# Attention and two mixers on one core: pairs 2 and 3 of q and k load into the buffers of pairs 0 and 1

## The chip, the core and the metric

The kernel runs on one core of one Trainium2 chip. The metric is device time in microseconds (us) of one launch, from setup to the last output byte. Before the change it is 679.75 us, the median of three runs (679.57 to 682.46). TensorE is called PE, VectorE DVE, ScalarE ACT, GpSimd POOL and SyncE SP, as in the profile.

## The reference

Three stages follow one another on an input of 4 batches, 8 heads, 576 positions and a head width of 64.

```python
# 1 attention: softmax over a sequence pooled by 4, plus softmax in a band
out_up    = np.repeat(sm_attn(q_d, k_d, v_d), 4, axis=2)    # q_d, k_d, v_d: means of 4 positions
out_local = np.matmul(softmax(where(abs(i - j) < 4, scale * q @ k.T, -1e9)), v)
x = out_up + out_local                                      # 4 x 576 x 512 when heads are joined
# 2 mixer: over positions, then over channels
u = x + (relu(x^T @ w_tok1) @ w_tok2)^T
x = u + relu(u @ w_ch1) @ w_ch2                             # 512 -> 1536 -> 512
# 3 mixer: a rotation by theta = x @ w_theta
y = w_tok_r @ (x * cos(theta)) + w_tok_i @ (x * sin(theta))
u = x + y;  result = u + relu(u @ w_ch)
```

## The kernel before

Two heads of one batch are a *pair*; pair n is batch n // 4 and heads 2(n % 4) and the next, so there are 16 pairs. Two pairs of a batch are a *quad* (eight of them). In tile names `qk_b_p` is the q and k of pair 4b + p.

For each pair the kernel loads q and k transposed (`load_pair`, L375, 582 KB, four buffers), pools them by 4 on DVE (`pool_pair`, L421 and L422), computes the band's scores on PE (`pair_local`: warm-up matmuls L315, mask L530, scores L533), takes the maximum and subtracts on DVE (L545, L546), exponentiates on ACT (L553), transposes on PE (L558), and multiplies with v (L568) and divides (L577 to L582). For each quad it pools v on POOL (`pool_values`, L396 loads it, L398 to L404 pool), computes pooled attention (`quad_front`: scores `sd` L434 and L443, maximum `mxd` L452 and L460, exponential `pd` L468 and L473, transposes `pdt` L477 and L482, product `od` L493 to L500, division L504 to L507), and writes the small result `ods` to DRAM and reads it back repeated (`od` L510, `ot` L511, then `xu` L516 and L519). L595 adds `xu` to the band's result `x`. The token mixer (`token_mix`, L598) follows for each quad. Weights arrive as 64-bit words, `raw`, and are cut into two 32-bit floats by ACT, DVE and POOL (`converted`, L187 to L223).

The attention and the token mixer take about the first 180 us; the channel mixer and the last stage fill the rest.

The order of the work is written out by hand. Each of the functions above is a generator that yields after a step; `ORDER` (L33) names one step after another, `P3` for the load of pair 3, `K3` for its pooling, `L3` for its band, `V1` and `F1` for quad 1, and so on, and each engine takes its instructions in that order. So SP also issues DMAs in that order, and a DMA that must wait for its buffer, or for one of eight completion semaphores that the loads take in turn, holds back every DMA behind it. The last stage, from L1136 on, is not in the table: there a scheduler sets the order, from its own estimate of when things are ready.

The four q-and-k buffers are taken in the order of the calls: pair 0, 1, 4 and 2 take one each, and pair 3, the fifth load, waits until pair 0 has been read by DVE and PE.

Of the kernel before, what the change touches and what calls it, by code (L numbers as in the profile page):

```python
# [12 lines left out]
F32 = mybir.dt.float32  # L13
# [17 lines left out]
FIRST = 1  # L31
ROWS = ((8, 9), (0, 2), (4, 6), (2, 3))
ORDER = """  # L33
G3 P0 G2 I*2 P1 G3 P4 G3 V0 P2 G3 K0 G3 G2 I G2 I L0*2 P3 K1 F0 W1 L0 F0 L1 L0 G3 F0 V0 L1*2 V0 L2 W0 G1 G0 G6 V1 G2
K2 V0 G2 F0 L1 F0 L2 K3 K4 L0 F0 L0 L2 L1 G2 F1 L2 L1 L0 F0 F1 G1*2 F1 V1 F0 P5 F0 W3 L0 F1 G5 G0 L1 G0 F1 K5 G6 F2 L1
G0 P6 W2 G5 G6 L3 V1 F2 V1 L3 G6 F2 F1 L3 G1 G4 F1 L2 P7 L5 L2 L5 F1 G1 L3 A0 V2 X0 A1 T0 L3 G1 L5 G0 L3 T0 G0 L2 G2
F1 G4 F2 G5 T0 K6 T0 V2 X2 L2 G6 W5 F2 K7 V2 L4*2 E0.0*2 T0 L4 V3 V2 A2 L3 E0.1 L5 G4 L4 W4 L5 G6 L5 G4 L3 X2 F3 G5 P8
P9 A3 G4 F2 G5 E0.1 T1 G4 G5 T0 F2 V3 L4 F3 F2 T0 L4 V3 X2 F3 L6 V3 L6 X7 T0 P11 L6 X2 X0 F3 K8 U0.0 L6 T0 X2 X0 U0.0
F3 L4 U0.0 V4 K9 F2 F3 X0 L6 L4 L6 T1 F4 U0.1 X0 F3 T1 L5 U0.1 X0 T1 U0.1 F4 X7 X4 V4 F3 T1 X7 F4 W6 L5 X7 E1.1 F4
E1.0 E1.1 L8 V4 L8 X7 E1.0 X1 A4 F4 T1 P10 A5 T1 X2 T2 L8 T1 U1.0*2 T2 T1 U1.0 X1 F3 L7 X7 L7 T2 X1 T2 X4 X5 K10 X1 L8  # L40
L6 U1.1*2 L7 T2 E2.0 U1.1 W7 X4 L7 V4 X1 L7 F4 W9 L7 L6 X4 E2.1 E2.0 C0 E2.1 T2 X1 L8 K11 X5 L7 T2 X5 L8 W8 L9*2 L7 X5
P13 T2 P12 L9 L10 C0 A6 F5 X4 C0 U2.0 L10 U2.0 X5 U2.0 C0 X3 F5 X6 F4 F5 C0 A7 F4 L10 T3 X4 F5 L9 V5 T3 H0.1 L8 U2.1
F5 T2 H0.1 H0.0 K12 T3 L9 U2.1 X5 C0 L9 U2.1 K13 F4 X6*2 L10 T3 X3 W13 H0.0 X6 H0.2 F6 E3.0*2 V5 P14 T3 F6 V5 H0.2 F6
C0 V6 V5 L8 X3 E3.1 L9 H0.3 F5 E3.1 X3 W10 L9 F6 X3 F5 L10 V6 A9 T3 F5 T3 V6 U3.0 L10 K14 T3 V6 U3.0 X6 U3.0 T3 H0.3
# [70 lines left out]
def kernel(  # L115
# [172 lines left out]
    sb1 = actx.enter_context(tc.tile_pool(name="a1", bufs=1))  # L288
    sb2 = actx.enter_context(tc.tile_pool(name="a2", bufs=2))
# [3 lines left out]
    def wide(name):  # L293
        return big.tile([128, 2, 512], F32, tag="big", name=name)
# [25 lines left out]
    def step(name, gen):  # L320
        gens[name] = gen
# [52 lines left out]

    def load_pair(n):  # L375
        b, p4 = divmod(n, 4)
        qk = sb2.tile([128, 2, S + 6], F32, tag="qk", name=f"qk_{b}_{p4}", bufs=4)
        sp.dma_start(qk, qkT[b, p4])
        loaded[n] = qk
        yield  # L380
# [141 lines left out]
    def pair_local(n):  # L522
# [426 lines left out]
    def lazily(f):  # L949
        yield from f()  # L950
# [190 lines left out]
    sb1 = ctx.enter_context(tc.tile_pool(name="c1p", reuse_waits="tile", bufs=1))  # L1141
    sb2 = ctx.enter_context(tc.tile_pool(name="c2p", reuse_waits="tile", bufs=2))
# [93 lines left out]
    T0, T1 = slice(0, HALF), slice(HALF, S)  # L1236
# [221 lines left out]
```

## Time and profile before

| What | Value |
|---|---|
| Runs | 679.75 us median of 3 (679.57, 679.75, 682.46) |
| Profiled execution | 679.18 us, span 677.4 us, mean granted PE clock 0.992 |
| PE busy | 655.6 us, 97% of the span |
| DVE busy | 519.8 us, 77% |
| ACT busy | 321.1 us, 47% |
| POOL busy | 100.1 us, 15% |
| DMA | 109.93 MB, mean 162 GB/s |
| First 101 us | PE busy 84.02, DVE busy 85.18, DMA engines 81% busy |

The profile is that of one execution. Start times are microseconds from the start of the span. A timeline row gives the start, the duration, the engine, the line, the operation and its tiles; in brackets stands the idle time before it and what ended that. "SPq" rows are the issue of a DMA, not its transfer: when a load landed is seen where an engine waited for it. PE's clock is given as a share of 2.4 GHz, so 0.50 is the lower of its two levels, 1.2 GHz. The page's shares are means over the whole span, and the change lies in the first 50 us, where no engine is busy all the time.

### The profile page before, as it was taken

The page shows a single profiled execution, that of the slowest core. Times are in us where ns is not written, and L with a number is a line of the kernel's source. Part 1 is how long each engine was busy: PE and PEld are TensorE (multiplying, and loading weights), DVE is VectorE, ACT ScalarE, POOL GpSimd, SP SyncE. Part 2 cuts the span into 40 slices and gives each one's busy share as a digit, 9 for nine tenths or more (in the row PEclk, how much of TensorE's full clock was granted, in tenths as well). Part 3 has the DMA queues.
Part 4 walks back from the last instruction along what each step waited for, and adds up shares of the span by engine and source line. Part 5 has one row for each costly group of instructions (what it writes and reads, how often), then busy time and mean ns, then how long its engine had stood idle before and what let it go on. Part 6 is the DMA issues. An engine that isn't in the chain of part 4 may idle for free.

```text
span 677.4 us, 17394 instructions
## 1 busy us (share of the span) xinstructions
PE 655.6 (97%) x7320; PEld 625.6 (92%) x7320; DVE 519.8 (77%) x952; ACT 321.1 (47%) x632; POOL 100.1 (15%) x92
## 2 busy tenths in 40 slices
PE   7779889999999999999999999999999999999997
PEld 4658879989999999999999999999999998998997
DVE  5989988697542888998987867677898748847837
ACT  3566758355342564535434523154647227427311
POOL 3224222415000423300101200012000000000000
PEclk8889999999999999999999999999999999999999
DMA  8797877757343685527263762699510330140202
GB/s 294 235 300 236 269 248 250 254 184 233 105 147 126 221 294 187 202 65 214 57 195 128 206 142 85 236 323 277 141 63 0 106 121 1 62 142 1 71 1 70
DMA packets 93021, 109.93 MB, mean 162 GB/s; under 512 B 46880, under 2 KB 69536, under 8 KB 92944
## 3 DMA queue, kind: packets, MB, share of 16 engines
q1 hardware_dynamic: 92080, 106.08, 49.4%
q0 software_dynamic: 864, 2.75, 1.1%
q8 instruction: 57, 0.93, 0.6%
q14 instruction: 20, 0.16, 0.1%
HBM read 79.13 MB, written 29.69 MB: 161 GB/s over the span
## 4 chain that ended last, share of the span: by engine, by line
PE 84%; DMA 5%; DVE 5%; SPq 2%; ACT 2%; issue 1%; DVEq 0%; ACTq 0%
PE y L157 6%; PE y L158 6%; PE y L159 6%; PE c L158 4%; PE c L157 4%; PE c L159 4%; PE c L699 4%; PE c L702 4%; PE c L700 4%; PE c_p L902 3%; PE c_p L905 3%; PE c_p L903 3%; PE th L158 2%; PE th L159 2%; PE th L157 2%; DMA qk<-qkT 2%
## 5 line engine op out<-in xcount | busy, mean ns | idle before, releaser
L158 PE MATMUL y<-wrl,zh 128*128 128x288 f32 x256 | 74.9, 296 | 0.0
L157 PE MATMUL y<-wrh,zh 128*128 128x288 f32 x256 | 74.8, 296 | 0.0
L159 PE MATMUL y<-wrh,zl 128*128 128x288 f32 x256 | 71.9, 295 | 0.0
L219 POOL TENSOR_TENSOR ww<-ww,raw 128x512 int32<-128x512 int32 (+2 forms) x30 | 41.0, 1373 | 160.1 <-DMA raw<-w_ch 52.9
L157 PEld LDWEIGHTS y<-wrh,zh 128*128 128x128 f32 x256 | 48.0, 188 | 0.0
L158 PEld LDWEIGHTS y<-wrl,zh 128*128 128x128 f32 x256 | 48.0, 188 | 0.0
L159 PEld LDWEIGHTS y<-wrh,zl 128*128 128x128 f32 x256 | 46.9, 188 | 0.0
L219 POOL TENSOR_TENSOR raw<-raw 128x512 int32<-128x512 int32 (+2 forms) x16 | 20.4, 1275 | 133.5 <-DVE raw L215 57.6
L1231 DVE TENSOR_TENSOR cx<-y,cx 128x288 f32<-128x288 f32 x32 | 14.6, 456 | 32.3 <-PE y L159 31.8
L151 ACT CAST cuh<-cx 128x288 fp32r<-128x288 f32 (+1 forms) x16 | 8.8, 553 | 59.6 <-DVE cx L1231 59.6
L199 ACT ACTIVATE ww<-raw 128x512 f32<-128x512 f32 (+2 forms) x30 | 19.5, 649 | 27.4 <-DVE c1l L223 9.5
L157 PE MATMUL th<-thh,cxh 128*128 128x512 f32 (+1 forms) x92 | 31.6, 343 | 0.0
L158 PE MATMUL th<-thl,cxh 128*128 128x512 f32 (+1 forms) x92 | 31.6, 343 | 0.0
L159 PE MATMUL th<-thh,cxl 128*128 128x512 f32 (+1 forms) x92 | 31.1, 343 | 0.0
L921 DVE SCALAR_TENSOR_TENSOR g<-c,g 128x384 fp32r<-128x384 f32 x40 | 21.1, 549 | 12.8 <-ACT g L918 12.8
L918 ACT ACTIVATE g<-c 128x384 fp32r<-128x384 f32 x40 | 19.2, 490 | 24.4 <-PE c L159 24.4
L201 ACT ACTIVATE raw<-raw 128x512 int32<-128x512 uint32 (+3 forms) x46 | 29.5, 641 | 0.0
L929 DVE TENSOR_TENSOR ut<-c,ut 128x384 f32<-128x384 f32 x32 | 17.1, 550 | 9.9 <-PE c L702 9.9
L568 PE MATMUL o<-vw,plt 38*32 38x65 f32 x1280 | 18.0, 231 | 3.8 <-issue 3.1
L157 PE MATMUL t<-w2h,h 128*128 128x256 f32 (+1 forms) x64 | 21.5, 337 | 0.0
L157 PE MATMUL c<-uh,c1h 128*128 128x384 f32 x64 | 21.4, 334 | 0.0
L159 PE MATMUL c<-uh,c1l 128*128 128x384 f32 x64 | 21.4, 334 | 0.0
(390 smaller groups left out, 2256.7 us busy)
## 6 DMA issues: line engine op xcount, KB each, us to landing
raw<-w_ch SPq DMA_DIRECT2D x27, 512.0 KB
qk<-qkT SPq DMA_DIRECT2D x16, 582.0 KB
xT<-ut SPq DMA_DIRECT2D x12, 768.0 KB
vd<-vtok SPq DMA_DIRECT2D x8, 650.0 KB
vw<-vloc SPq DMA_DIRECT2D x32, 146.2 KB
uT<-us SPq DMA_DIRECT2D x16, 288.0 KB
ut<-uT SPq DMA_DIRECT2D x6, 768.0 KB
ut<-xT SPq DMA_DIRECT2D x6, 768.0 KB
```

The costliest lines, as they stand in the source:

```text
L157: pe.matmul(out, lh, rh, start=start, stop=False, skip_group_check=again)
L158: pe.matmul(out, lh, rl, start=False, stop=False, skip_group_check=again)
L159: pe.matmul(out, ll, rh, start=False, stop=stop, skip_group_check=again)
L201: act.activation(f, words[:, :, 0], AF.Copy, scale=2.0**-29)
L219: pool.tensor_tensor(out=w.bitcast(I32), in0=w.bitcast(I32), in1=f, op=ALU.add)
L699: pe.matmul(ps[:, 0:MIX], h[:, cb % 2, d], h1, start=cb == cbs[0], stop=False)
L700: pe.matmul(ps[:, 0:MIX], l[:, cb % 2, d], h1, start=False, stop=False)
L702: pe.matmul(ps[:, 0:MIX], weight[cb // 2][2][:, cb % 2, d], h2, start=False, stop=cb == cbs[-1])
L902: pe.matmul(ps[:, 0:MIX], h[:, cb % 2, d], h1, start=cb == cbs[0], stop=False)
L903: pe.matmul(ps[:, 0:MIX], l[:, cb % 2, d], h1, start=False, stop=False)
L905: pe.matmul(ps[:, 0:MIX], weight[cb // 2][2][:, cb % 2, d], h2, start=False, stop=cb == cbs[-1])
L921: dve.scalar_tensor_tensor(out=h2, in0=ps, scalar=0.0, in1=h1.bitcast(F32), op0=ALU.max, op1=ALU.subtract)
```

## The change

The q-and-k buffers become four tiles of their own, and a table says which pair uses which. Pairs 2 and 3 now use the buffers of pairs 0 and 1; pairs 4 and 5 use the other two, which nothing used before them. The table of steps is changed with it, in its first lines only.

```diff
-G3 P0 G2 I*2 P1 G3 P4 G3 V0 P2 G3 K0 G3 G2 I G2 I L0*2 P3 K1 F0 W1 L0 F0 ...
+G3 P0 G2 I*2 P1 G3*2 V0 G3 K0 G3 G2 I G2 I L0*2 P2 W0 G1 K1 F0 L0 F0 L1 L0 G3 F0 V0 L1 P3 G0 W1 ...
...
+QK = (0, 1, 0, 1, 2, 3, 0, 1, 3, 2, 3, 0, 2, 1, 3, 0)
...
-        qk = sb2.tile([128, 2, S + 6], F32, tag="qk", name=f"qk_{b}_{p4}", bufs=4)
+        qk = sb1.tile([128, 2, S + 6], F32, tag=f"qk{QK[n]}", name=f"qk_{b}_{p4}")
```

Line numbers of the kernel after are one higher from L92 on. The first place is SP's start, before: `qk_0_1` is pair 1, `qk_1_0` pair 4, `vd` the v of a quad, `vw` the v of a pair's band, `raw` a weight.

```order
L378 DMA qk_0_1_148<-qkT 128x1164
L378 DMA qk_1_0_152<-qkT 128x1164
L396 DMA vd_0_0_157<-vtok 128x1300
L378 DMA qk_0_2_159<-qkT 128x1164
L378 DMA qk_0_3_240<-qkT 128x1164
L387 DMA vw_0_1_266<-vloc 32x1170 x2
L387 DMA vw_0_1_266<-vloc 6x1170 x2
L387 DMA vw_0_0_364<-vloc 32x1170 x2
L387 DMA vw_0_0_364<-vloc 6x1170 x2
L187 DMA raw_2_369<-w_tok1 128x2x256
L187 DMA raw_3_371<-w_tok1 128x2x256
```

And the same stretch of SP after:

```order
L379 DMA qk_0_1_148<-qkT 128x1164
L397 DMA vd_0_0_155<-vtok 128x1300
L379 DMA qk_0_2_236<-qkT 128x1164
L388 DMA vw_0_0_238<-vloc 32x1170 x2
L388 DMA vw_0_0_238<-vloc 6x1170 x2
L188 DMA raw_2_243<-w_tok1 128x2x256
L379 DMA qk_0_3_342<-qkT 128x1164
L188 DMA raw_3_344<-w_tok1 128x2x256
L388 DMA vw_0_1_346<-vloc 32x1170 x2
L388 DMA vw_0_1_346<-vloc 6x1170 x2
```

Pair 4 is gone from behind pair 1. Pair 2 now waits for the readers of pair 0, and pair 3 for those of pair 1, with `raw_3` and `vw_0_1` behind it.

The second place is SP at the first pooled result, `od` and `ot` out and `xu` back in, before:

```order
L396 DMA vd_0_1_375<-vtok 128x1300
L510 DMA od_0_0_57<-ods_0_0_567 4x32x256
L511 DMA ot_0_0_65<-ods_0_0_567 4x32x64
L378 DMA qk_1_1_589<-qkT 128x1164
L516 DMA xu_0_0_591<-od_0_0_57 128x1x1024
L519 DMA xu_0_0_591<-ot_0_0_65 64x1x256 x2
L387 DMA vw_0_3_595<-vloc 32x1170 x2
```

And after:

```order
L511 DMA od_0_0_57<-ods_0_0_557 4x32x256
L512 DMA ot_0_0_65<-ods_0_0_557 4x32x64
L397 DMA vd_0_1_578<-vtok 128x1300
L517 DMA xu_0_0_580<-od_0_0_57 128x1x1024
L520 DMA xu_0_0_580<-ot_0_0_65 64x1x256 x2
L379 DMA qk_1_0_585<-qkT 128x1164
L379 DMA qk_1_1_587<-qkT 128x1164
L188 DMA raw_4_589<-w_tok2 128x288
L388 DMA vw_0_3_591<-vloc 32x1170 x2
```

Pairs 4 and 5 and `raw_4` are now issued behind `xu`, and `xu` waits for `od` to reach DRAM. At the second pooled result the same is done to pair 7 (`qk_1_3`), the v of quad 2 and a weight, all now behind `xu_0_1`.

The third place is DVE behind the band result of pair 1 (`x_0_0`), before; `qa` and `qkd` are the two adds of a pooling.

```order
L421 TENSOR_TENSOR qa_1_1_670<-qk_1_1_589 128x576
L422 TENSOR_TENSOR qkd_1_0_446<-qa_1_1_670 128x288
L577 TENSOR_SCALAR rl_0_1_697<-o_0_1_623 128x10
L578 RECIPROCAL rl_0_1_697<-rl_0_1_697 128x10
L582 TENSOR_TENSOR x_0_0_603<-o_0_1_623,rl_0_1_697 128x2x5x64
L203 TENSOR_SCALAR ww_4_673<-ww_4_673 128x288
L206 TENSOR_SCALAR ww_4_673<-ww_4_673 128x288
L215 SCALAR_TENSOR_TENSOR ww_4_673<-raw_4_373,ww_4_673 128x288
L452 TENSOR_REDUCE mxd_1_0_732<-sd_1_0_676 128x4
L460 TENSOR_REDUCE mxd_1_0_732<-sd_1_0_676 64x1 x2
L545 TENSOR_REDUCE mx_0_3_816<-s_0_3_715 128x10
```

And after:

```order
L583 TENSOR_TENSOR x_0_0_599<-o_0_1_619,rl_0_1_669 128x2x5x64
L422 TENSOR_TENSOR qa_1_0_674<-qk_1_0_585 128x576
L423 TENSOR_TENSOR qkd_1_0_673<-qa_1_0_674 128x288
L422 TENSOR_TENSOR qa_1_1_677<-qk_1_1_587 128x576
L423 TENSOR_TENSOR qkd_1_0_673<-qa_1_1_677 128x288
L204 TENSOR_SCALAR ww_4_666<-ww_4_666 128x288
L207 TENSOR_SCALAR ww_4_666<-ww_4_666 128x288
L216 SCALAR_TENSOR_TENSOR ww_4_666<-raw_4_589,ww_4_666 128x288
L546 TENSOR_REDUCE mx_0_3_783<-s_0_3_694 128x10
```

Both poolings of quad 2 stand together behind `x_0_0`; pair 4's stood between those of pair 3 and `mx_0_2`. The maximum of quad 2 (`mxd_1_0`) moves behind the low half of `x_0_0` (L606, `xl_0_0`), its scores on PE behind the transposes of pair 3, and its exponential on ACT behind `raw_6`.

## Rows read from the trace of the kernel before

**Rows 1.** Windows: busy time and count by engine, PE clock, DMA share, GB/s

```profile
0.00:101.00 101.00, 84.02 (x2451) 67.62 (x2452) 85.18 (x164) 60.41 (x142) 32.95 (x35) 0.95 0.81 263
101.00:677.40 576.40, 571.56 (x4870) 557.98 (x4870) 434.65 (x789) 260.74 (x490) 67.13 (x57) 1.00 0.46 145
```

**Rows 2.** Timeline of DVE, 4 to 11 us: start, duration, work, idle before

```profile
5.63 1.19 DVE L421 TENSOR_TENSOR qa<-qk 128x576 f32<-128x576 f32 x1 [0.37 <-DMA qk<-qkT]
...
7.88 0.43 DVE L215 SCALAR_TENSOR_TENSOR raw<-raw 128x256 uint32<-128x256 uint32 x1
...
9.54 0.76 DVE L421 TENSOR_TENSOR qa<-qk 128x576 f32<-128x576 f32 x1 [1.24 <-DMA qk<-qkT]
```

**Rows 3.** Timeline of SP, 0 to 46 us: issues of DMAs

```profile
1.20 0.42 SPq L378 DMA_DIRECT2D qk<-qkT  x1
...
3.53 0.91 SPq L378 DMA_DIRECT2D qk<-qkT  x2
...
23.12 0.62 SPq L510 DMA_DIRECT2D od<-ods  x1
...
29.59 2.79 SPq L387 DMA_DIRECT2D vw<-vloc  x4
...
32.42 0.35 SPq L187 DMA_DIRECT2D raw<-w_tok  x1
...
38.06 0.58 SPq L510 DMA_DIRECT2D od<-ods  x1
...
44.22 1.20 SPq L519 DMA_DIRECT2D xu<-ot  x2
```

**Rows 4.** Timeline of PE, 11 to 18 us

```profile
11.99 2.89 PE L315 MATMUL s<-zero 128*128 128x320 bf16 x12
...
15.82 1.80 PE L315 MATMUL s<-zero 128*128 128x320 bf16 x12
```

**Rows 5.** Windows, columns as in group 1

```profile
12.00:14.00 2.00, 2.00 (x10) 1.18 (x9) 1.86 (x4) 1.02 (x4) 1.34 (x1) 0.50 1.02 368
```

**Rows 6.** Timeline of DVE, 18 to 23 us

```profile
18.25 0.76 DVE L421 TENSOR_TENSOR qa<-qk 128x576 f32<-128x576 f32 x1
...
20.71 0.55 DVE L545 TENSOR_REDUCE mx<-s 128x10 f32<-128x380 f32 x1
```

**Rows 7.** Timeline of DVE, 29 to 51 us

```profile
29.51 0.75 DVE L421 TENSOR_TENSOR qa<-qk 128x576 f32<-128x576 f32 x1
30.30 1.44 DVE L422 TENSOR_TENSOR qkd<-qa 128x288 f32<-128x288 f32 x1
...
32.84 0.38 DVE L203 TENSOR_SCALAR ww<-ww 128x288 f32<-128x288 f32 x1
...
33.98 0.75 DVE L452 TENSOR_REDUCE mxd<-sd 128x4 f32<-128x576 f32 x1
...
35.83 0.56 DVE L545 TENSOR_REDUCE mx<-s 128x10 f32<-128x380 f32 x1 [0.57 <-PE s L533]
...
40.17 0.69 DVE L223 TENSOR_TENSOR w1l<-raw,w1h 128x512 fp32r<-128x512 f32 x1 [0.67 <-ACT w1h L221]
...
45.00 0.75 DVE L421 TENSOR_TENSOR qa<-qk 128x576 f32<-128x576 f32 x1
45.79 1.63 DVE L422 TENSOR_TENSOR qkd<-qa 128x288 f32<-128x288 f32 x1
...
48.52 0.83 DVE L421 TENSOR_TENSOR qa<-qk 128x576 f32<-128x576 f32 x1
...
50.32 0.42 DVE L643 SCALAR_TENSOR_TENSOR h<-t,h 128x256 fp32r<-128x256 f32 x1 [0.48 <-ACT h L640]
```

**Rows 8.** Timeline of POOL, 45 to 47 us

```profile
45.77 1.34 POOL L398 TENSOR_TENSOR vd<-vd 128x650 f32<-128x650 f32 x1 [9.52 <-DMA vd<-vtok]
```

**Rows 9.** Timeline of ACT, 30 to 36 us

```profile
35.09 0.48 ACT L199 ACTIVATE ww<-raw 128x288 f32<-128x288 f32 x1 [4.25 <-DMA raw<-w_tok]
```

**Rows 10.** Chain that ended last, a load of one pair later on

```profile
127.51 7.42 DMA qk<-qkT
```

More of the change, by code (lines that the diff above doesn't have):

```diff
@@ L33 @@
 ORDER = """
[L34 to L41, printed above, removed]
+G3 P0 G2 I*2 P1 G3*2 V0 G3 K0 G3 G2 I G2 I L0*2 P2 W0 G1 K1 F0 L0 F0 L1 L0 G3 F0 V0 L1 P3 G0 W1 L1 V0 L2 G2 K2 V0 G2
+F0 L1 F0 L2 K3 L0 F0 L0 L2 L1 G2 F1 L2 L1 L0 F0 F1 G1*2 F1 F0 V1 F0 V1 P4 P5 G6 W3 L0 F1 G5 G0 L1 G0 F1 G6 L1 K4 K5 G0
+P6 W2 G5 G6 L3 V1*2 L3 G6 F1 L3 G1 G4 F1 L2 L5 L2 L5 F1 G1 L3 A0 A1 T0 L3 F2 G1 L5 G0 L3 T0 F2 G0 L2 G2 F1 P7 V2 G4 F2
+G5 T0 F2 K6 T0 V2 X2 L2 G6 W5 F2 K7 V2 L4*2 E0.0*2 T0 L4 V3 V2 A2 L3 E0.1 L5 G4 L4 X0 W4 L5 G6 L5 G4 L3 X2 F3 G5 P8 P9
+A3 G4 F2 G5 E0.1 T1 G4 G5 T0 F2 V3 L4 F3 F2 T0 L4 V3 X2 F3 L6 V3 L6 X7 T0 P11 L6 X2 X0 F3 K8 U0.0 L6 T0 X2 X0 U0.0 F3
+L4 U0.0 V4 K9 F2 F3 X0 L6 L4 L6 T1 F4 U0.1 X0 F3 T1 L5 U0.1 X0 T1 U0.1 F4 X7 X4 V4 F3 T1 X7 F4 W6 L5 X7 E1.1 F4 E1.0
+E1.1 L8 V4 L8 X7 E1.0 X1 A4 F4 T1 P10 A5 T1 X2 T2 L8 T1 U1.0*2 T2 T1 U1.0 X1 F3 L7 X7 L7 T2 X1 T2 X4 X5 K10 X1 L8 L6
+U1.1*2 L7 T2 E2.0 U1.1 W7 X4 L7 V4 X1 L7 F4 W9 L7 L6 X4 E2.1 E2.0 C0 E2.1 T2 X1 L8 K11 X5 L7 T2 X5 L8 W8 L9*2 L7 X5
 P13 T2 P12 L9 L10 C0 A6 F5 X4 C0 U2.0 L10 U2.0 X5 U2.0 C0 X3 F5 X6 F4 F5 C0 A7 F4 L10 T3 X4 F5 L9 V5 T3 H0.1 L8 U2.1
```

## The prediction, made before the changed kernel ran

> **What bounds the kernel now.** First the windows on both sides of 101 us [rows 1]. From 101 us to the end PE is busy for 571.56 of 576.40 us: what comes after starts as soon as it can and goes at PE's pace. Before 101 us PE is busy for 84.02 us and DVE for 85.18. So the kernel's time is the moment at which PE gets through the attention plus a fixed stretch, and the change lies ahead of that moment. There the timelines count. DVE is the one to follow: the reader sees it work one instruction behind another, with short gaps, each closed by a load, by PE or by ACT [rows 2, 6, 7]. SP's issues tell when a load could start [rows 3]; when it landed is seen where DVE or ACT waits for it. I follow DVE to 50 us, and carry the shift found there to the end: after it nothing in the order differs in the rest of the attention, DMAs, DVE, ACT and PE wait for one another, and a common delay finds no slack to end in.
>
> The sum is made against the profiled execution, 679.18 us for a span of 677.4. That is 0.57 us under the median of 679.75, less than the spread of the runs; I do not correct for it.
>
> **The change step by step.** "Pooling" is the two adds of one pair on DVE.
>
> 1. Pair 4's load no longer moves beside pair 1's. Pair 1 was issued from 3.53 us, and DVE, free at 7.88 + 0.43 = 8.31, began its pooling at 9.54 when it landed [rows 2, 3]. The gain lies between 0 and 1.2 us. The v load still moves beside it, so I take half: 0.6.
>
> 2. PE's warm-up matmuls for pair 1 follow the pooled scores and so that pooling. The twelve took 2.89 us at a granted clock of 0.50; the next twelve took 1.80 [rows 4, 5]. The clock had fallen while PE waited for the pooling. With a shorter wait it may stay up: a gain of 0 to 1.1; I take 0.5. Pair 1's scores then end at 15.82 - 1.1 = 14.7.
>
> 3. Pair 3's load now waits for them, and behind it on SP wait `raw_3`, the v of pair 1 and the store of the pooled result. How long a load of 582 KB takes: pair 0, with loads about it, 1.20 to 5.63, or 4.43 us [rows 2, 3]. A weight of half the size, nearly alone, took 2.67 (32.42 to 35.09) [rows 3, 9]; a pair in heavy traffic later took 7.42 [rows 10]. 4.43 is nearest, as a weight moves ahead and one behind. Pair 3 lands at 19.1, not before 18.25 when its pooling ran. Two poolings took from 18.25 to 20.71, 1.23 each [rows 6]; one of them, pair 4's, is now elsewhere. The maximum that follows starts at 19.1 + 1.2 = 20.3 in place of 20.71: of 1.1 us gained and 1.2 us of work moved off, 0.4 is left.
>
> 4. The store of the pooled result goes from 23.12 to 22.7. From there to the issue that followed `xu` were 29.59 - 23.12 = 6.47 us, a round trip through DRAM [rows 3]. In that place now stand pairs 4 and 5: issued at 29.2 and 29.7, landed at 33.6 and 34.1.
>
> 5. DVE comes to them early. It finished `x_0_0` at 32.84; less 0.4, less pair 5's pooling that stood ahead (29.51 to 31.74, its second add slowed to 1.44) is 30.2 [rows 7]. It waits 3.4 us. Two poolings, 2.5 us, end at 36.1; the weight's three instructions take 1.14 (32.84 to 33.98); the next maximum starts at 37.2, not 35.83: 1.4 late. The maximum of quad 2 that stood between (33.98 to 35.26, 1.28 us) is not ahead of it any more.
>
> 6. That one comes in before pair 6's pooling: 45.00 + 1.4 + 1.3. The idle 0.67 before L223 at 40.17 is filled: 47.0, or 2.0 late [rows 7].
>
> 7. The second add of pair 6 took 1.63 us, beside POOL's pooling of v at 45.77 [rows 7, 8]; that of pair 3 or 4 at most 0.5. Its v now lands some 6 us later, so POOL is idle here: 1.1 back, 0.9 late.
>
> The Trainium skill, in "SBUF — State Buffer", section "SBUF: two separate sides", says that VectorE and GpSimd share a port pair under an exclusive lock, and that whoever comes second is blocked. By it POOL's pooling will block some other DVE instruction when it does run. The trace has DVE busy for most of this stretch, so there is little idle time for it to fall in. The sum by the rule would be 1.1 us higher, 681.8.
>
> 8. Pair 7's load now stands behind the second `xu`. From the store at 38.06 to the end of `xu`'s issues were 7.4 us [rows 3]. With less traffic I take the 6.4 of the first: 38.06 + 1.4 + 6.4 + 4.4 = 50.3, and DVE is ready at 48.52 + 0.9 = 49.4. A wait of 0.9 (0 to 1.9), of which 0.48 fills an idle gap behind it [rows 7]: 1.4 late in the end.
>
> The other moves I cost at nothing. Quad 1's v is issued 4 us later, and quad 2's; POOL had waited 9.52 us for one like it, PE needs the result several us on, and if that cover is gone each us late is one on PE. Two weights change places in X0 and X2. The scheduler's order on PE in the last stage changes too, but there PE has under 5 us of gaps in all [rows 1], and neither a gain nor a loss above 1 us can come of it.
>
> Sum: 679.18 + 1.4 = 680.6 us.
>
> **The rivals.**
>
> *The loads are hidden.* They land in 2.67 us and the clock stays up. Pair 1's pooling starts at 8.5 and its scores end at 13.7, 2.1 early. Pair 3 lands at 16.4, ahead of its turn. The store goes at 21.0, pairs 4 and 5 land at 30.2 and 30.7, DVE needs them at about 30: poolings, weight and next maximum at 33.9, 1.9 early. Steps 6 and 7 add 0.6 and take 1.1; pair 7 is in time. About 2.4 early: 676.8. For it: DMA is 81% busy, not full [rows 1], and each load moved leaves room for one that is needed. Against it: three loads of this size show 4.4 us or more.
>
> *Loads go strictly in turn.* If what is issued behind pair 1 does not slow it, step 1 and 2 give nothing. Scores end at 15.8, pair 3 lands at 20.2, the maximum is 0.7 late, pairs 4 and 5 land 1.1 later than in the forecast, and steps 5 to 8 bring 2.5: 681.7. For it: pair 0's load, with little behind it, took 4.43 too. Against it: pair 1's took 6.0, with more behind it than ahead [rows 2, 3].
>
> The Trainium skill, in "DMA: Bandwidth & Descriptors", section "Queues, rings and completion order", says that each DMA engine takes the descriptors of a queue in ring order. By that rule this is the case to expect. It also says that a later one may finish before an earlier one; the 6.0 us of pair 1 beside 4.43 of pair 0 leave it open.
>
> *Pairs 4 and 5 land late.* Mechanism: `xu` waits for DRAM, SP stands, then `xu`, both pairs, a weight and four v loads go out within 5 us. If the pair takes the 7.42 us of the row later on [rows 10], it lands at 36.6. DVE has nothing else to do in its order. Each us there is a us at the end, from the moment the load takes more than about 1 us; past 7.0 us the kernel is slower by over 0.5%. At 7.42 it is 3.0 more than the forecast: 683.6. For it: that row moved 582 KB among other DMAs as here. Against it: step 4's neighbours are fewer, and pair 0 shows 4.43.
>
> **How the numbers follow.** Forecast 680.6: 0.43. Hidden, 676.8: 0.20. In turn, 681.7: 0.22. Late, 683.6: 0.15. About 0.5%, or 3.4 us, is what a measurement of this kernel can tell from no change; the bounds are 676.35 and 683.15. The hidden case with more gained, for instance where PE stood for an issue, falls below: 0.08. Above fall most of the late case and a corner of the in-turn case: 0.15. The rest, 0.77, is no change. The range for 8 in 10 runs from 676.6, a little beyond the hidden case, to 683.8, a little beyond the late one. The forecast's own range, from the bounds in steps 1, 2 and 8, is 679 to 682.5.
>
> **What would show it right or wrong.** In the changed profile DVE's pooling of pair 1 should start near 8.9 (step 1), the second twelve warm-up matmuls show whether the clock fell (2), DVE should wait for pair 3 near 19 (3), and wait 2 to 4 us near 31 for pair 4 (4, 5); a pooling of pair 6 near 46 to 47 whose second add takes 0.5 (6, 7); a short wait for pair 7 (8). PE should be shifted by one amount from 50 us on. The prediction is wrong in its core if DVE does not wait for pairs 4 and 5, or if the shift at 50 us is not the shift at the end.

## The result: 0.8% slower, and the profile after

The kernel after takes 685.63 us, the median of 12 runs (683.52 to 691.13); the kernel before, run beside it, 680.51 (12 runs, 675.66 to 683.92). The ratio is 1.0079, with a 95% interval of 1.0054 to 1.0104. That is 5.4 us more on 680.5, where 1.4 was forecast, and beyond the end of the range.

The profiled execution took 683.77 us, for a span of 682.0. The first fence is DVE's timeline after, up to 56 us; it answers to [rows 2, 6, 7]. In brackets is the idle time ahead and what ended it.

```profile
9.62 0.76 DVE L422 TENSOR_TENSOR qa<-qk 128x576 f32<-128x576 f32 x1 [1.37 <-DMA qk<-qkT]
...
14.88 0.55 DVE L546 TENSOR_REDUCE mx<-s 128x10 f32<-128x380 f32 x1 [1.14 <-PE s L534]
...
18.84 0.76 DVE L422 TENSOR_TENSOR qa<-qk 128x576 f32<-128x576 f32 x1 [1.66 <-DMA qk<-qkT]
...
33.93 0.76 DVE L422 TENSOR_TENSOR qa<-qk 128x576 f32<-128x576 f32 x1 [2.82 <-DMA qk<-qkT]
...
36.19 0.76 DVE L422 TENSOR_TENSOR qa<-qk 128x576 f32<-128x576 f32 x1 [1.01 <-DMA qk<-qkT]
...
38.80 0.55 DVE L546 TENSOR_REDUCE mx<-s 128x10 f32<-128x380 f32 x1
...
50.08 0.46 DVE L423 TENSOR_TENSOR qkd<-qa 128x288 f32<-128x288 f32 x1
...
51.77 0.75 DVE L422 TENSOR_TENSOR qa<-qk 128x576 f32<-128x576 f32 x1
...
55.71 0.42 DVE L644 SCALAR_TENSOR_TENSOR h<-t,h 128x256 fp32r<-128x256 f32 x1 [2.71 <-ACT h L641]
```

DVE stands for pair 3 (1.66 us), pair 4 (2.82) and pair 5 (1.01). `mx_0_3` starts at 38.80, where it was 35.83 [rows 7], and the h of pair 1's token mixer at 55.71, where it was 50.32. Why the loads are late is seen on SP and in the windows, which answer to [rows 3] and [rows 5].

```profile
22.56 0.61 SPq L511 DMA_DIRECT2D od<-ods  x1
...
26.39 0.62 SPq L517 DMA_DIRECT2D xu<-od  x1
27.10 1.23 SPq L520 DMA_DIRECT2D xu<-ot  x2
28.38 1.05 SPq L379 DMA_DIRECT2D qk<-qkT  x2
29.47 0.43 SPq L188 DMA_DIRECT2D raw<-w_tok  x1
29.95 2.55 SPq L388 DMA_DIRECT2D vw<-vloc  x4
```

```profile
22.00:24.00 2.00, 1.79 (x91) 1.38 (x89) 1.15 (x3) 1.72 (x4) 0.00 (x0) 1.00 0.04 7
...
32.00:34.00 2.00, 2.00 (x124) 1.60 (x125) 0.07 (x1) 0.00 (x0) 0.87 (x2) 1.00 1.00 384
```

From 22 to 24 us the DMA engines move 7 GB/s (the last column): SP stands first for the store of the pooled result, then for its way through DRAM, and all loads are behind it. Before the change the same stretch was full:

```profile
22.00:24.00 2.00, 2.00 (x64) 1.60 (x61) 1.20 (x5) 1.74 (x5) 0.00 (x0) 1.00 1.03 400
```

Then ten DMAs go out within 6.1 us (26.39 to 32.50), and the engines are full (1.00). Pairs 4 and 5 land 5.5 and 7.2 us after their issue (28.38 to 33.93; 29.0 to 36.19). `raw_4`, of half the size, takes longer still, in the timeline of ACT:

```profile
37.25 0.46 ACT L200 ACTIVATE ww<-raw 128x288 f32<-128x288 f32 x1 [7.79 <-DMA raw<-w_tok]
```

DVE's steps on that weight stand ahead of `mx_0_3`, so the chain of work that ended last runs from the store through `raw_4`, which came 0.3 us behind pair 5's pooling:

```profile
22.56 3.81 DMA od<-ods
...
29.47 7.75 DMA raw<-w_tok
37.25 0.47 ACT ww L200
...
38.89 0.47 DVE mx L546
```

The burst repeats. In the five profiles that have it (two executions of the kernel after, and `x4`, `x7` and `x9` below) pair 4 lands 5.1 to 5.6 us after its issue, pair 5 7.1 to 7.7 and `raw_4` 7.6 to 8.2.

One profile is one execution, so both kernels were profiled once more. The times are those of DVE, but for the issue of the store (SP); the last column is the difference of the means.

| us | before | before again | after | after again | after − before |
|---|---|---|---|---|---|
| pooling of pair 1 | 9.54 | 8.60 | 9.62 | 8.63 | +0.1 |
| store of the first pooled result issued | 23.12 | 22.57 | 22.56 | 24.63 | +0.8 |
| from there to `mx_0_3` | 12.71 | 13.48 | 16.24 | 16.14 | +3.1 |
| from `mx_0_3` to h of pair 1 | 14.49 | 14.68 | 16.91 | 16.46 | +2.1 |
| from there to the start of the channel mixer (`ul`) | 48.72 | 50.59 | 47.67 | 47.37 | −2.1 |
| from there to the span's end | 578.36 | 578.38 | 578.62 | 578.90 | +0.4 |
| span | 677.4 | 679.7 | 682.0 | 683.5 | +4.2 |

The first execution of before, which the prediction was worked from, took 679.18 us, the other 681.50. The loss is there at h, 6.0 us (0.8 + 3.1 + 2.1), and 2.1 of it come back by the start of the channel mixer. Its first load (`ut`) stands behind other loads, and DVE, which makes the low half of it (`ul`), waited for it before and hardly does after:

```profile
99.04 1.76 DVE L681 TENSOR_TENSOR ul<-ut,uh 128x1536 fp32r<-128x1536 f32 x1 [1.99 <-ACT uh L679]
```
```profile
103.38 1.76 DVE L682 TENSOR_TENSOR ul<-ut,uh 128x1536 fp32r<-128x1536 f32 x1 [0.35 <-ACT uh L680]
```

### The profile page after: what moved, and what is told of

It reads as the page before. It is cut to its first block, busy times and chain, and to the rows that moved or that the text cites. A ratio compares the mean times of both kernels' runs of the same rounds, so it can differ in the third digit from the quotient of the medians.

```text
span 682.0 us, 17390 instructions
## 1 busy us (share of the span) xinstructions
PE 657.8 (96%) x7320; PEld 627.6 (92%) x7320; DVE 518.7 (76%) x952; ACT 321.2 (47%) x632; POOL 98.3 (14%) x92
## 4 chain that ended last, share of the span: by engine, by line
PE 83%; DMA 6%; DVE 5%; ACT 3%; SPq 1%; issue 1%; DVEq 0%; ACTq 0%
PE y L158 6%; PE y L159 6%; PE y L160 6%; PE c L159 4%; PE c L158 4%; PE c L160 4%; PE c L700 4%; PE c L701 4%; PE c L703 4%; PE c_p L903 3%; PE c_p L906 3%; PE c_p L904 3%; PE th L159 2%; PE th L160 2%; PE th L158 2%; DMA qk<-qkT 2%
## 5 line engine op out<-in xcount | busy, mean ns | idle before, releaser
L159 PE MATMUL c<-ul,c1h 128*128 128x384 f32 x64 | 21.4, 334 | 0.0
```

What stands on the lines that cost most here:

```text
L159: pe.matmul(out, lh, rl, start=False, stop=False, skip_group_check=again)
```

## The experiments

16 kernels ran, and the kernels before and after once more for a second profile. A ratio is to the kernel before, run on the same chip, with its 95% interval; the kernel after has 1.0079 (1.0054 to 1.0104). In the runs `x1`, `x3` and `x4` line numbers are 49 lower. In the diffs stand the steps of the order table around the edit: P is the load of a pair, K its pooling, W its v; V and F are a quad's v and pooled branch, G a weight (`G6` is `raw_4`, `G0` `raw_3`).

| Run | What it is | Ratio |
|---|---|---|
| x1_loads_ahead | after; pairs 4, 5, `raw_4` ahead of the store | 1.0031 (1.0008 to 1.0055) |
| x11_loads_in_hole | after; the same between store and reload, ahead of `vd_0_1` | 1.0057 (1.0021 to 1.0094) |
| x20_behind_vd | after; the same, behind `vd_0_1` | 1.0042 (1.0014 to 1.0069) |
| x17_pair4_early | after; pair 4 loaded and pooled early | 1.0063 (1.0033 to 1.0092) |
| x15_pair4_late | before; pair 4 loaded and pooled late | 1.0039 (1.0007 to 1.0071) |
| x3_quad2_only | before; quad 2 in its new place | 1.0007 (0.9981 to 1.0032) |
| x9_quad2_back | after; quad 2 in its old place | 1.0132 (1.0086 to 1.0178) |
| x4_late_only | after; pairs 2 and 3 wait for no buffer | 1.0063 (1.0036 to 1.0090) |
| x7_clock_held | after; 30 more throwaway products | 1.0097 (1.0075 to 1.0119) |
| x5_free_and_ahead | x4 and x1 together | 1.0059 (1.0025 to 1.0093) |
| x10_free_old_order | early loads, DVE's order of before | 1.0087 (1.0053 to 1.0122) |
| x12_hole_quad2 | x11; quad 2 back | 1.0077 (1.0042 to 1.0112) |
| x21_both | x20; pair 3 last of its group | 1.0094 (1.0060 to 1.0127) |
| x22_pair7_back | x20; pair 7 and `vd_1_0` back | 1.0085 (1.0063 to 1.0106) |
| x23_pair7_quad2 | x22; quad 2 back | 1.0086 (1.0052 to 1.0119) |
| x14_before_mix_early | before; first load of the channel mixer sooner | 1.0079 (1.0050 to 1.0108) |
| x0_before_again, x13_after_again | one execution each, in the table above | |

### Are the late loads the cause?

```diff
-V0 L1 P3 G0 W1 L1 V0 ... F0 V1 F0 V1 P4 P5 G6 W3
+V0 L1 P3 G0 W1 P4 P5 G6 L1 V0 ... F0 V1 F0 V1 W3
```

> The changed kernel, with three issues of SP moved: the loads of pairs 4 and 5 and of the weight slice raw_4 stand right behind the load of vw_0_1, ahead of the store of pooled results (od), instead of behind the two loads of xu that wait for it. In the changed kernel these three were issued at 28.4 to 29.5 us and landed 5.5, 7.3 and 7.75 us later, while the DMA engines had moved 7 GB/s at 22 to 24 us; the token mixer's x was ready for pair 6 at 56 us, 5.4 us later than before. Late loads: they are now issued at about 22 us, land before DVE and ACT ask at 31 us, DVE waits for none of them, mx_0_3 comes at 34.5 to 35.5, the h of pair 1's token mixer is on DVE at 50 to 51 us, and the run takes 4 to 5.5 us less than the changed kernel (679.5 to 681 beside 685). Quad 2's new place: its exponential on ACT and its transposes on PE still stand ahead of the token mixer, so 2 to 3 us stay and the run is 682 to 683. The clock: PE no longer idles 4.9 us ahead of pair 3's scores, so its granted clock stays at 1.00 from 38 to 54 us, which is where it was 0.50.

The ratio fell from 1.0079 to 1.0031, 3.3 us of 5.4 at the middle of the intervals. DVE waits for neither pair any more, but for pair 3 longer: first SP's issue of pair 3, then DVE.

```profile
13.52 0.36 SPq L330 DMA_DIRECT2D qk<-qkT  x1
```
```profile
20.01 0.76 DVE L373 TENSOR_TENSOR qa<-qk 128x576 f32<-128x576 f32 x1 [4.19 <-DMA qk<-qkT]
...
33.77 0.80 DVE L373 TENSOR_TENSOR qa<-qk 128x576 f32<-128x576 f32 x1
```

Pair 3 lands 6.5 us after its issue, not 4.0. So the late loads are a cause and, at the middle of the intervals, the larger part of the loss. Whether in this place they also delay pair 3 isn't shown: without them it took 7.14 us in the second execution of the kernel after. The hole behind the store looked better:

```diff
-F1 F0 V1 F0 V1 P4 P5 G6 W3
+F1 F0 P4 P5 G6 V1 F0 V1 W3
```

> The changed kernel with one edit in SP's order: the loads of pairs 4 and 5 and of raw_4 stand between the store of pooled results and its reload (xu), ahead of vd_0_1, instead of behind the reload, so that they fill the stretch at 23 to 27 us in which SP stands for the store. Unlike the run with these loads ahead of the store, they can't take transfer time from pair 3, which has landed by then. The hole: pairs 4 and 5 are issued at about 24 to 25 us, land by 29 to 30, DVE's waits of 2.82 and 1.01 us go, mx_0_3 comes 13 to 14 us behind the store instead of 16.2, and the run is 680.5 to 682, level with the kernel before. If the late loads were not the cause, the run stays within 0.3% of the changed kernel's 685.6.

It gained nothing that can be told. DVE doesn't wait for pairs 4 and 5, but `vd_0_1` now comes behind them, and POOL's work (its add of `vd_0_1`, then a step on a weight that stands behind it) runs beside the poolings. First POOL, then DVE:

```profile
34.29 1.34 POOL L399 TENSOR_TENSOR vd<-vd 128x650 f32<-128x650 f32 x1 [20.62 <-DMA vd<-vtok]
35.59 1.50 POOL L220 TENSOR_TENSOR raw<-raw 128x512 int32<-128x512 int32 x1
```
```profile
34.39 1.56 DVE L423 TENSOR_TENSOR qkd<-qa 128x288 f32<-128x288 f32 x1
35.98 1.72 DVE L422 TENSOR_TENSOR qa<-qk 128x576 f32<-128x576 f32 x1
```

DVE's two adds take 1.56 and 1.72 us; in the kernel after, where POOL is through by then, 0.46 and 0.76. It is step 7 in the other direction, and here the rule that the prediction cites from the Trainium skill ("SBUF — State Buffer", section "SBUF: two separate sides") does what it says. So the next one leaves `vd_0_1` in front:

```diff
-F1 F0 V1 F0 V1 P4 P5 G6 W3
+F1 F0 V1 P4 P5 G6 F0 V1 W3
```

> The changed kernel with the loads of pairs 4 and 5 and raw_4 between the store and its reload, but behind vd_0_1, which keeps its place right behind the store. In the run with them ahead of vd_0_1 DVE's waits went, and POOL's adds of vd_0_1 fell beside the pooling instead (34.3 to 39.1 us). Late loads and POOL: POOL's adds run at 28 to 33 us again, the pooling of pairs 4 and 5 starts at 32 to 34 us without a wait of over 1 us and takes 0.46 us for each second add, mx_0_3 comes 13.5 to 14.5 us behind the store, and the run gains 2 to 3 us over the changed kernel. If the order behind the store doesn't count, it stays within 0.25% of the changed kernel.

`mx_0_3` comes 13.06 us behind the store (22.75 to 35.81), as before the change (12.71 and 13.48). The ratio, 1.0042, is 2.5 us better than after at the middle of intervals that overlap. Behind `mx_0_3` DVE now stands for pair 7, whose load the change had put behind the second reload:

```profile
35.81 0.55 DVE L546 TENSOR_REDUCE mx<-s 128x10 f32<-128x380 f32 x1
...
53.01 0.76 DVE L422 TENSOR_TENSOR qa<-qk 128x576 f32<-128x576 f32 x1 [3.81 <-DMA qk<-qkT]
```

Pair 7's load and `vd_1_0`'s put back to where they were, on top of that:

```diff
-F1 L2 L5 L2 L5 F1 G1 L3 A0 A1 ... G2 F1 P7 V2 G4 F2
+F1 L2 P7 L5 L2 L5 F1 G1 L3 A0 V2 A1 ... G2 F1 G4 F2
```

> The run with the loads of pairs 4 and 5 and raw_4 behind vd_0_1, with pair 7's load and vd_1_0's put back to where the kernel before had them: pair 7 ahead of the second store of pooled results, vd_1_0 right behind it, instead of behind the second reload. Pair 7's place: DVE's wait of 3.81 us goes, h of pair 1 comes 16.3 to 16.9 us behind mx_0_3, at 52 to 53 us, and the run gains 1 to 2 us on the one before it (682.5 to 684, the kernel before plus 0.1 to 0.3%); what is left is quad 2's place. A version that beats the kernel before is not expected. If each load that is moved forward makes another one late, the run stays at 0.35 to 0.6% above the kernel before.

Worse, not better. DVE no longer waits for pair 7, but the second store, issued at 40.68, has its reload at 47.60, 6.9 us later, where it was 5.5 (38.06 to 43.53) before, with these two loads in the same places, and 3.5 after (40.79 to 44.25). h came at 56.27, 19.6 us behind `mx_0_3` (36.70), where it was 18.4 in `x20`. So taking that wait away did not bring back what `x20` was left with. The last expectation of the text held in kind (the reload is late in place of pair 7's load), but the run is above the 0.35 to 0.6% that it gave.

### Which part of the change makes them late?

Pair 4's place alone, in the kernel before:

```diff
-P1 G3 P4 G3 V0 P2 ... K3 K4 L0 ... V1 F0 P5 F0 W3 ... F1 K5 G6 F2
+P1 G3*2 V0 P2 ... K3 L0 ... V1 F0 P4 P5 F0 W3 ... F1 K4 K5 G6 F2
```

> The kernel before with one part of the change: pair 4's load goes out with pair 5's, between the store of pooled results and its reload, and pair 4 is pooled right ahead of pair 5, instead of early. Pairs 0 to 3 then have a buffer each, so that no load of q and k waits for a buffer up to there; all else is as before. Pair 4's place: DVE has 1.24 us more to do from the first reload to mx_0_3, pair 5 lands later behind pair 4, and the run takes 1.5 to 3 us more than the kernel before (683.5 to 685). Reused buffers: the loss of the changed kernel comes from pairs 2 and 3, which wait for nothing here, and the run is within 0.15% of the kernel before.

1.0039: half of the loss, with no buffer to wait for. But in its profile DVE waits for neither of the two loads. PE shows why it is slower, first at pair 2's scores, then at quad 2's, which are still in their old place:

```profile
22.65 0.26 PE L533 MATMUL s<-qk 64*32 64x38 f32 x4 [2.80 <-issue]
...
36.29 0.48 PE L434 MATMUL sd<-qkd 64*32 64x144 f32 x16 [2.28 <-DVE qkd L422]
...
38.22 0.73 PE L434 MATMUL sd<-qkd 64*32 64x144 f32 x16 [1.22 <-DVE qkd L422]
...
39.41 3.38 PE L315 MATMUL s<-zero 128*128 128x320 bf16 x12
```

PE stood 2.80 us for nothing the profile names, and the store went at 26.93, some 4 us later than before. Then PE stood for the poolings of pairs 4 and 5, now one behind the other, its granted clock fell to 0.50, and the twelve warm-up products for pair 3 took 3.38 us. `mx_0_3` came 17.3 us behind the store (44.22). In this profile, then, it is pair 4's pooling in its late place, ahead of quad 2, that is waited for, and not a late load. And the other way round, pair 4's load and pooling put back in the kernel after:

```diff
-P1 G3*2 V0 ... K3 L0 F0 L0 L2 L1 ... V1 P4 P5 G6 W3 ... G6 L1 K4 K5 G0
+P1 G3 P4 G3 V0 ... K3 K4 L0 F0 L0 L2 L1 ... V1 P5 G6 W3 ... G6 L1 K5 G0
```

> The changed kernel with pair 4 back where it was: its load right behind pair 1's (its buffer, 2, is free from the start) and its pooling ahead of mx_0_2. Pairs 2 and 3 still wait for the buffers of pairs 0 and 1, pair 5 and raw_4 still go out behind the reload. Pair 4's place: mx_0_3 comes 13.5 to 14.5 us behind the store instead of 16.2, and the run gains 2 to 3 us over the changed kernel (682.5 to 683.5). Reused buffers: pair 3 still lands 4 to 7 us after its issue at about 14 us, the store comes at 23.5 to 24.6 as in the changed kernel, and 2 us of its loss stay; if all of it comes from there, the run stays at 685.

1.0063, not told from the kernel after. Pair 4 no longer waits, and DVE stands for pair 5 alone, 4.90 us:

```profile
36.37 0.76 DVE L422 TENSOR_TENSOR qa<-qk 128x576 f32<-128x576 f32 x1 [4.90 <-DMA qk<-qkT]
```

So either part is enough to lose: pair 4 late costs 0.4% in the kernel before, and with pair 4 early in the kernel after 0.6% stay, with pair 5 and `raw_4` behind the reload and the rest of the change. The two don't split the 0.8%, since by the profiles they work through different waits. What is left in x1 and x20 (0.3 and 0.4%) isn't split either, and `raw_4`, through which the chain after runs, was not moved alone.

### The waits for buffers

```diff
-... K0 G3 G2 I G2 I L0*2 P2 W0 ... V0 L1 P3 G0 W1
+... V0 P2 P3 G3 K0 G3 G2 I G2 I L0*2 W0 ... V0 L1 G0 W1
-QK = (0, 1, 0, 1, 2, 3, ...
+QK = (0, 1, 2, 3, 0, 1, ...
```

> The changed kernel with other buffers for q and k, so that pairs 0 to 3 have one each and the loads of pairs 2 and 3 wait for nothing; they are issued right behind vd_0_0. Pairs 4 and 5 and raw_4 keep their place behind the loads of xu. This takes away the waits by which the change is named and leaves the place of the later loads. Late loads: no gain worth the name, pairs 4 and 5 are issued at 27 to 29 us and land at 33 to 37, and the run stays 3 to 5 us above the kernel before (683 to 685). If the reuse of the buffers of pairs 0 and 1 were the cause, the run would go back to the kernel before's time, 680 to 681.

1.0063, not told from the kernel after. The late loads are there without the waits for buffers, and `mx_0_3` still comes 16.3 us behind the store (23.70 to 40.03):

```profile
35.00 0.76 DVE L373 TENSOR_TENSOR qa<-qk 128x576 f32<-128x576 f32 x1 [2.06 <-DMA qk<-qkT]
...
37.50 0.76 DVE L373 TENSOR_TENSOR qa<-qk 128x576 f32<-128x576 f32 x1 [1.25 <-DMA qk<-qkT]
```

So the waits that give the change its name cost nothing that these runs can tell. With the loads of pairs 4 and 5 and `raw_4` moved ahead of the store as well, as in x1:

```diff
-V0 L1 G0 W1 L1 V0 ... F0 V1 F0 V1 P4 P5 G6 W3
+V0 L1 G0 W1 P4 P5 G6 L1 V0 ... F0 V1 F0 V1 W3
```

> The changed kernel with both of its waits and its late loads taken away: pairs 0 to 3 have a buffer each and the loads of pairs 2 and 3 go out behind vd_0_0, and pairs 4, 5 and raw_4 go out ahead of the store of pooled results. Quad 2 and the pooling of pairs 4 and 5 keep their new places. Late loads: pair 3 no longer lands late as it did when pairs 4 and 5 went out right behind it (6.5 us after its issue, with 4.19 us of DVE's wait), DVE waits for no load up to 35 us, mx_0_3 comes 12.5 to 14 us behind the issue of the store instead of 16.2, and the run is within 0.3% of the kernel before. Quad 2's new place: from mx_0_3 to the h of pair 1 it is still 16.3 to 16.9 us, where it was 14.5 before, so the run stays 1.5 to 2.5 us above the kernel before.

No better than x1 (1.0059). On top of it, pair 4 early too, and the poolings of pairs 4 and 5 and quad 2 as in the kernel before (quad 2's edit is that of x9 below):

```diff
-L0*2 W0 G1 ... W1 P4 P5 G6 L1 ... K3 L0 ... F1 G6 L1 K4 K5 G0
+L0*2 P4 W0 G1 ... W1 P5 G6 L1 ... K3 K4 L0 ... F1 K5 G6 F2 L1 G0
```

> A version meant to beat both: DVE's order and quad 2's place as in the kernel before, the loads of pairs 2, 3 and 4 early (buffers 2, 3 and, once pair 0 is pooled, 0) and pair 5 and raw_4 ahead of the store of pooled results, pair 7's as in the changed kernel. If the kernel before loses time only by loads, it gains the 0.67 and 0.57 us that DVE waits there: 679 to 680 beside 681. If those waits are PE's and ACT's, it is the kernel before within 0.2%. It would be slower only if pair 4's early load delays pair 1 or pair 2.

0.9% slower than the kernel before, with its DVE order and earlier loads. PE shows a part of it, in the scores of pairs 1 and 2, 80 products each:

```profile
14.65 0.31 PE L534 MATMUL s<-qk 64*32 64x38 f32 x17 [1.30 <-issue]
...
21.31 0.26 PE L534 MATMUL s<-qk 64*32 64x38 f32 x4 [2.53 <-issue]
```

It stops in the middle, 1.30 and 2.53 us, for nothing the profile names; the last section comes back to it. And pair 3 as the last load of its group, on top of x20:

```diff
-L1 P3 G0 W1 L1 V0
+L1 G0 W1 P3 L1 V0
```

> The run with the loads behind vd_0_1, and one edit more: raw_3 and vw_0_1 are issued ahead of pair 3's load instead of behind it, so that they go out at 12 to 14 us, while SP waited for pair 1's buffer, and nothing is issued behind pair 3 until the store. Loads in flight share the engines: pair 3, last of its group, lands when the group is through, at 19 to 21 us as in the profiles with the longer wait, so that nothing is gained over the run without this edit, 0 to 0.5 us. Loads go in turn: pair 3 then lands later than in the changed kernel's first profile (18.8), at 20 to 21, and the run loses 1 to 2 us. If the wait of SP is what keeps the queue empty, pair 3 lands at 17.5 to 18.5 and the run gains 1 to 2 us.

Pair 3, issued at 15.89, is pooled at 23.43, 7.5 us behind its issue and later than any of the expectations had it, and the run is 3.5 us slower than x20. What was issued ahead of it seems to move first or beside it.

### Quad 2's place and the clock

Quad 2's steps alone, in the kernel before:

```diff
-G6 F2 L1 G0 P6 ... V1 F2 V1 L3 G6 F2 F1 ... T0 L3 G1 L5 G0 L3 T0 G0 ... G5 T0 K6
+G6 L1 G0 P6 ... V1 V1 L3 G6 F1 ... T0 L3 F2 G1 L5 G0 L3 T0 F2 G0 ... G5 T0 F2 K6
```

> The kernel before, loads and buffers untouched, with one part of the change: the pooled scores, the maximum, the exponential and the transposes of quad 2 (a batch's third pair in the pooled branch) stand at the places that the changed kernel gives them, behind the first steps of pair 1's token mixer, instead of ahead of pair 6's pooling. Late loads: with all loads landing as before these moves cost 0 to 0.5 us, the run is the kernel before's 680 within 0.1%. Quad 2's new place: the chain from DVE's maximum over ACT's exponential to PE's transposes now stands ahead of the token mixer's first matrix products; h of pair 1 is on DVE 1.5 to 2.7 us later than at 50.3, and the run takes that much longer (681.5 to 683). My prediction put +2.0 us on this move in the order of DVE alone.

From `mx_0_3` to h it takes 18.5 us (36.19 to 54.73), 4.0 more than before, and yet the run is level: h isn't the moment that sets the end. Put back in the kernel after:

```diff
-K4 K5 G0 P6 ... V1*2 L3 G6 F1 ... T0 L3 F2 G1 L5 G0 L3 T0 F2 G0 ... G5 T0 F2 K6
+K4 K5 F2 G0 P6 ... V1 F2 V1 L3 G6 F2 F1 ... T0 L3 G1 L5 G0 L3 T0 G0 ... G5 T0 K6
```

> The changed kernel with quad 2's pooled scores, maximum and exponential put back to where they were, right behind the pooling of pair 5 and ahead of pair 1's token mixer; all loads stay where the change put them, so pairs 4, 5 and raw_4 land late. Quad 2's new place: from mx_0_3 to the h of pair 1 it is again 14.5 us and the run gains 2 us or more over the changed kernel (683 to 684 beside 685.5). Late loads: quad 2 waits for the same late loads, its maximum now stands ahead of mx_0_3 and moves it by 1.4 to 2, so what is gained behind it is lost ahead of it, and the run stays within 0.8 us of the changed kernel.

1.0132, 0.5% more than after at the middle of intervals that overlap a little: PE stands at quad 2's scores until pairs 4 and 5 are there, and `mx_0_3` waits behind it.

```profile
44.20 0.55 DVE L546 TENSOR_REDUCE mx<-s 128x10 f32<-128x380 f32 x1 [3.34 <-PE s L534]
```

The same edit on top of x11, and on top of x22:

> The same as the run with the loads between the store and its reload, with quad 2 put back as well: its pooled scores, maximum and exponential right behind pair 5's pooling. With the loads late this cost 3.6 us more, since PE stood at quad 2's scores ahead of pair 3's. Late loads: with the loads in time it costs nothing, and the run is within 0.3% of the one without it. Quad 2's new place: it takes 2 us off from mx_0_3 to the h of pair 1, and the run is 679 to 680.5. If PE's order is what counts, not the loads, it is slower by 2 us or more again.

> The run with pair 7's load put back, and quad 2 back too, right behind pair 5's pooling; pairs 2 and 3 still reuse the buffers of pairs 0 and 1, and pair 4 is still pooled with pair 5. Quad 2's new place: 2 us less from mx_0_3 to h, as between 16.5 in the changed kernel and 14.5 in the kernel before, and the run gains 1 to 2 us (level with the kernel before). Loads: quad 2's maximum stands ahead of mx_0_3 again and moves it by 1.4 to 2 us, and nothing is gained, within 0.2%.

Neither differs from its partner without it (1.0077 and 1.0057; 1.0086 and 1.0085). Quad 2's new place moves work from ahead of `mx_0_3` to behind it and by itself costs nothing that these runs can tell. For the clock, one line behind the transposes of a pair:

```diff
+        warm(pt[:, 1, 192:512], 30 if n == 2 else 0)
```

> The changed kernel with 30 more throwaway products on PE behind the transposes of pair 2's q and k (into an unused part of the same bank), about 1.8 us at full clock or 3.6 at half, in the stretch from 35 to 40 us in which PE waits 4.86 us for pair 3. It takes no load and no wait away; it only leaves PE less idle. The clock counts: the granted clock stays at 1.00 (or comes back sooner) from 38 to 54 us, pair 3's transposes take 0.8 us instead of 1.33, those of quad 2 0.7 instead of 1.33, and h of pair 1 comes 2 to 3 us sooner than at 55.7; the run takes 2 to 3 us less than the changed kernel. Late loads alone: the products of this stretch hide beside the chain of waits over ACT and DVE, and the run stays within 0.7 us of the changed kernel (684 to 686).

First two windows of this run, then one of the kernel after:

```profile
40.00:42.00 2.00, 1.16 (x9) 0.60 (x7) 1.90 (x6) 0.16 (x1) 0.89 (x2) 1.00 0.99 276
44.00:46.00 2.00, 0.77 (x5) 0.53 (x5) 1.87 (x4) 2.00 (x4) 0.00 (x0) 1.00 0.29 83
```
```profile
40.00:42.00 2.00, 1.57 (x82) 1.12 (x82) 1.93 (x5) 2.00 (x6) 1.07 (x1) 0.50 0.65 198
```

The 30 products took 4.24 us, not the 1.8 of the expectation. The clock stayed at 1.00 up to 46 us, where the kernel after had 0.50 from 38 us on, and nothing came of it: from the store to h it took 32.97 us (24.61 to 57.58), in the kernel after 33.15. From 48 to 56 us it was 0.50 here too, so a clock held there was not tried.

### A try 60 us further on, and the second profiles

In the kernel before, from the wait for `ut` seen above:

```diff
-U1.1 W7 X4 ... E2.1 E2.0 C0 E2.1
+U1.1 C0 W7 X4 ... E2.1 E2.0 E2.1
```

> The kernel before with one load moved 60 us behind the change: the first load of the mixing stage (ut) stands right behind the store it reads, ahead of eight loads of v (vw) that were issued from 86.5 to 90.7 us. In the kernel before it lands 6.76 us after its issue at 90.75 and DVE waits 1.99 us for it at 99.0, where the last stage begins; in the changed kernel that wait is 0.35, so that up to 1.6 us of its loss may vanish there. If that load sets the start of the last stage, the run takes 1 to 2 us less than the kernel before; if PE's own work up to 98.3 us does, 0 to 0.7.

0.8% slower. The load must wait until the store it reads has landed, and twelve loads of v stand behind it. The chain of waits has it:

```profile
88.34 4.29 DMA uT<-us
92.66 0.37 SPq L672
...
93.08 6.30 DMA vw<-vloc
```

The second profiles, whose numbers stand in the first table:

> The kernel before, unchanged, profiled once more, since the execution that the prediction was worked from is below the median of its runs (679.2 us beside 680.5 to 681.9). If executions of one program differ early on, pair 1's landing is not 9.54 again but somewhere from 8.3 to 9.8, as in four executions of kernels whose first 8 us of issues are alike; the load of pair 5, mx_0_3 and the h of pair 1 then stand up to 2 us from their 29.5, 35.8 and 50.3, and the difference of single profiles is to be read with that doubt. If the profile repeats, they stand within 0.3 us.

> The changed kernel, unchanged, profiled once more, to see which of its differences return. The late loads: pairs 4 and 5 are issued behind the reload again and DVE waits 3 us or more for them in all; the DMA engines move under 50 GB/s in a stretch of 2 us between the loads of vw_0_1 and the reload; mx_0_3 comes 16 to 16.5 us behind the issue of the store and the h of pair 1 16.3 to 17.2 us behind mx_0_3. Pair 1's landing is expected to differ (8.3 to 9.8 us).

Up to 20 us the executions of one program differ by 1 us and more, and before's second one had lost its lead by `mx_0_3` (36.05 beside 35.83). The late loads returned in the second execution after, and pair 3 was later still:

```profile
13.90 0.36 SPq L379 DMA_DIRECT2D qk<-qkT  x1
```
```profile
21.04 0.76 DVE L422 TENSOR_TENSOR qa<-qk 128x576 f32<-128x576 f32 x1 [4.83 <-DMA qk<-qkT]
```

No version beat the kernel before.

## Why the prediction was wrong, step by step

- **Step 1**, 0.6 from pair 1's landing: not there. The means are 9.07 before and 9.13 after, and one program spreads over 1 us.
- **Step 2**, the clock: the twelve warm-up products took 1.80 us after, as hoped, but so did they in before's second execution (at 11.03). The term was an accident of one profile.
- **Step 3**, pair 3: 4.43 us was taken for its landing; it took 3.96 and 7.14 in two executions of the same program, 6.5 and 7.5 in x1 and x21. In the nine profiles with the same loads in the same order up to there it took 4.0 to 7.2. The store went at 22.56, as forecast (22.7), and at 24.63.
- **Steps 4 and 5 are the ones that failed.** The order of things was right: SP's hole, the issues at 28.4 (29.2 forecast), DVE's wait ahead of `mx_0_3`. The time to land was not: 5.5 and 7.2 us in place of 4.43. I left the 7.42 of [rows 10] to a rival, and took pair 0's row as the nearest, though the rows of pairs 0 and 1 and [rows 10] are all of one size and show 4.43, 6.0 and 7.42. The likely reason for the longer time is what goes out with it: here ten DMAs within 6.1 us, after a hole. Pair 4 came at 33.93, near the 33.6 forecast, since it was issued 0.8 us sooner; pair 5 came at 36.19, 2.1 us after its 34.1. `raw_4`, whose landing I didn't follow at all, took 7.75 and came last. In place of 1.4 us late, `mx_0_3` was 3.0 late, and 4.7 between the two second executions.
- **Step 6**, quad 2: 0.6 us was forecast, and with steps 7 and 8 nothing in all from `mx_0_3` to h. It was 2.1 us more, but x3 shows no cost in the run's time.
- **Step 7**: pair 6's second add takes 0.46 us after, as forecast, but it did so in before's second execution too. The 1.63 of [rows 7] was, like step 2, an accident of one profile:

```profile
46.13 0.46 DVE L422 TENSOR_TENSOR qkd<-qa 128x288 f32<-128x288 f32 x1
```

- **Step 8**, pair 7: no wait after, since DVE was later than forecast; 3.81 us in x20, where it was not.
- **The shift at 50 us was to be the shift at the end.** It isn't: of 6.0 us at h, 2.1 are back at the start of the channel mixer. The prediction named this as a sign that its core is wrong.
- **The sums**: step 8 adds up to 1.3, and the sum by the rule in step 7 to 681.7. Neither 0.1 matters.
- **The base.** The sum stood on an execution 1.3 us under the median of the 12 runs that followed.

The rival "Pairs 4 and 5 land late", with 683.6 us and a chance of 0.15, had the mechanism and, for pair 5, nearly the time to land (7.42). That its end, 4.4 us up on its base, comes near the measured 5.4 is in part luck: it had neither the 2.1 us at quad 2 nor the 2.1 us that come back. "The loads are hidden" is out. "Loads go strictly in turn" is neither: pair 3 landed 2.5 us later with two loads behind it (x1), but 3.2 us later also without them (after again).

What stays open: the intervals are 0.2 to 0.5 points wide on each side, so what pair 4's place and the loads behind the reload cost is known no finer than given. Why the same program lands pair 3 in 4.0 or 7.1 us wasn't found.

## What to carry to other kernels

A load issued behind an instruction that waits for a round trip leaves the DMA engines idle and then meets everything else that waited: price it by the worst landing seen in such a burst, not by a load of the same size in lighter traffic, and follow every load of the burst, the small one too. A load moved forward in a full stretch can make another one late, so count the one that is late next. And profile the kernel before twice before a term of 1 us is believed.

## What the runs showed of the hardware

PE stops in mid-stream, where the profile names nothing that it waits for. In the scores of pairs 1 and 2 the stops stand at the same product in every profile that has them, 17 before the end of pair 1's 80 and 4 before the end of pair 2's, and between the two lie 128 products (17 + 12 + 2 + 5 + 16 + 76). The page counts a queue of its own for code, here before:

```profile
q8 instruction: 57, 0.93, 0.6%
```

0.93 MB in 57 packets is 16 KB each, and the page counts their time as a share of the same 16 engines that move the data. From 9 to 50 us the stops add up to 3.9 and 6.1 us in the two executions before, 0.2 and 2.0 after; in x10 the two shown are 3.8, and in x15 one alone is 2.80. They need not cost time at the end: x3's profile has 8.7 us of them, and the run is level with before. That a stop is a code packet behind data is argued from the fixed distance, not shown.
